# A recurrent attention feeding a two-layer MLP on one core: low input halves by a matmul with minus the identity, late checks in halves and spread out, a third output buffer

## The chip, the cores and the metric

The kernel runs on one core of a Trainium2 chip. The metric is the device time of one execution in microseconds (us). The engines are named as in the profile: PE (TensorE matmuls; PEld its weight loads), DVE (VectorE), ACT (ScalarE), POOL (GpSimd) and SP (the queue that issues all DMAs here).

## The reference

```python
def _attn_ref(r, k, v, w, u):                 # each of r, k, v, w: (4, 8, 768, 48); u: (8, 48)
    state = zeros((B, H, D, D))
    for t in range(S):
        cur = einsum('bhd,bhe->bhde', u[None] * kt, vt)
        y[:, :, t] = einsum('bhd,bhde->bhe', rt, state + cur)
        state = wt[:, :, :, None] * state + einsum('bhd,bhe->bhde', kt, vt)
    return y

def _moe_ref(x, w_in, w_out, alpha):          # x: (3072, 384), w_in: (384, 2048), w_out: (2048, 384)
    h = x @ w_in
    g = maximum(h, 0) + alpha * minimum(h, 0)
    return g @ w_out
```

The attention output, rows of 8 heads by 48, is the x of the MLP.

## The kernel before

The sequence is cut into 6 chunks of 128 steps for each of 4 batches, 24 chunks q in all. For a chunk, `prep` makes running products of the decays w on DVE (two scans, L359 and L365) and scales k and r with them (L368, L371); `scores` multiplies them on PE (L422), DVE lays the products below the diagonal into a tile `at` (L427, copy_predicated), whose diagonal ACT has written (L398); `outputs` adds the part of the carried state (L509) and `at` times v (L464), and updates the state (L471). The chunk's output, transposed, lies in a PSUM bank `yp`.

Three chunks make a group of 384 tokens, whose inputs x must be split in two 32-bit reduced-precision tiles, high and low, so that three products (high by high, low by high, high by low) give nearly full precision. `take` in `outputs` does this: ACT casts `yp` to the high tile (L484), DVE subtracts the high tile from `yp` to get the low one (L486). For groups after the first a part of 128 columns, `x3s`, is split in the same way and moved into place by six small DMAs (L538).

The MLP runs in steps. A step n takes one tile j of 128 hidden columns for one group: nine matmuls "up" (L588) into a bank; ACT scales (L592, "pos"), DVE combines (L594), ACT casts the high half (L596, "gh"), DVE the low half (L597, "gl"); two steps later (LAG = 2) nine matmuls "down" (L606), three each for the three chunks, add to PSUM tiles `op0` to `op2`. The weights are loaded as 16 tiles `raw`, and each is rebuilt and split into `wh` and `wl` by two ACT and four DVE instructions (L561, L563, L566, L569, L572, L574). There are 8 groups by 16 tiles, 128 steps. The first three groups run the tiles 0 to CUT - 1 first, and the rest later, so that work on PE begins before all weights are made; their partial sums go to DRAM (`part`) and are read back and added by L619.

The checks that the fast path may be used read all decays again (12 loads, L677; one ACT instruction each, L679) and all weights again (16 loads, L686; two ACT instructions each, L688 and L689). The sums of the last two come with a short extra instruction that reads the accumulator. They share the ring of two `raw` buffers. Their result is one number, read at the end.

What stands on each engine, and in which order, is decided when the kernel is built. `Plan.op` records each piece of work with an engine, an estimated duration, the tiles it reads and writes and, for some, a due time; `Plan.order` goes through time with these estimates and gives each free engine the ready piece with the earliest due time; buffers come from rings of fixed length. On the chip each engine then runs its list strictly in this order, waiting where data is late. `PLACE` says before which steps the chunks of the first three groups are due, `STEP` and `ATT` what a step and a chunk are taken to cost in the due times.

At the end, `moe_out` copies `op0` to `op2` of the last group to tiles `os` (a ring of two; ACT for s = 0 and 2, DVE for s = 1) and sends each to DRAM (L628):

```python
                os_ = Tensor(r_os)
                ...
                    op("ACT", 0.41, lambda s=s, os_=os_: nc.scalar.copy(out=os_.ap, in_=ops_[s]),
                       r=[("op", s)], w=[os_], due=due_step[n] + STEP)
```

## Time and profile before

| | us |
|---|---|
| median of 3 runs | 556.07 (553.01 to 557.01) |
| the profiled execution's own time | 559.03 |
| span of the profiled execution, first to last instruction | 557.3 |
| PE busy in the span | 527.0 (95%) |
| DVE busy | 356.4 (64%) |
| ACT busy | 311.7 (56%) |
| POOL busy | 60.0 (11%) |
| mean granted PE clock | 0.974 of full |

Busy time is a mean over a span whose stages differ, and PE's matmuls overlap each other, so a high share does not say that PE never waited. What a stage is bound by is read from that stage: which engine is without a gap there, and which wait of PE ends last.

### The profile page before, as it was taken

The numbers are of one execution on the slowest core, as the hardware profiler recorded it, in microseconds if no ns is written. First come the engines' busy times: TensorE is split into PE (matmuls) and PEld (weight loads), VectorE is DVE, ScalarE is ACT, GpSimd is POOL, SyncE is SP. The second block draws the span as 40 slices with busy tenths as digits, with TensorE's granted clock in tenths as the row PEclk, the third lists the DMA queues.
The fourth block names the chain that finished last, engine by engine and source line by source line (L and its number), as shares of the span: only waits on it lengthen the run. The fifth ranks groups of instructions, "written<-read, shape, count | busy, mean of one in ns | idle before, by whom it ended". The sixth has DMA issues, their size and how long they took to land.

```text
span 557.3 us, 9687 instructions
## 1 busy us (share of the span) xinstructions
PE 527.0 (95%) x3724; PEld 507.2 (91%) x3724; DVE 356.4 (64%) x604; ACT 311.7 (56%) x720; POOL 60.0 (11%) x74
## 2 busy tenths in 40 slices
PE   6977888999999999989999999999999999999993
PEld 6866777999999899979999999999999999999993
DVE  7999999999997464655646376466484434333331
ACT  3865665856667878687745545445454443333331
POOL 2002315410002010020100110110000000000000
PEclk9788998999999999989999999999999999999998
DMA  8666565655557878777604232223121100000001
GB/s 310 207 219 208 180 202 177 223 168 167 196 168 239 287 247 303 240 265 254 209 0 107 66 102 77 85 70 103 58 74 23 42 1 2 18 19 29 0 2 48
DMA packets 29655, 75.14 MB, mean 135 GB/s; under 512 B 4064, under 2 KB 10912, under 8 KB 29600
## 3 DMA queue, kind: packets, MB, share of 16 engines
q1 hardware_dynamic: 29600, 74.44, 41.2%
q8 instruction: 31, 0.51, 0.4%
q14 instruction: 24, 0.20, 0.1%
HBM read 65.87 MB, written 6.49 MB: 130 GB/s over the span
## 4 chain that ended last, share of the span: by engine, by line
PE 69%; DMA 11%; DVE 10%; ACT 5%; issue 2%; SPq 1%; DVEq 0%; ACTq 0%
PE bank L588 30%; PE op L606 29%; DMA raw<-in_wts_dram 7%; PE bank L422 3%; PE bank L464 2%; PE bank L509 2%; DMA out_dram<-os 2%; DVE wd L365 1%; ACT at L398 1%; DVE suf L359 1%; PE bank L471 1%; ACT raw L689 1%; DVE raw L569 1%; DMA u_dm<-in_u_dram 1%; DVE at L427 1%
## 5 line engine op out<-in xcount | busy, mean ns | idle before, releaser
L588 PE MATMUL bank<-x,wh 128*128 128x384 f32 x768 | 224.5, 347 | 1.7 <-ACT wh L572 0.9
L588 PEld LDWEIGHTS bank<-x,wh 128*128 128x128 f32 x768 | 143.7, 191 | 5.0 <-ACT wh L572 1.5
L592 ACT ACTIVATE pos<-bank,alpha_n 128x384 f32<-128x384 f32 x128 | 74.4, 581 | 120.1 <-PE bank L588 120.0
L606 PE MATMUL op<-wh,gh 128*128 128x384 f32 x384 | 132.4, 345 | 3.4 <-ACT gh L596 2.4
L588 PE MATMUL bank<-x,wl 128*128 128x384 f32 x384 | 132.1, 344 | 2.3 <-DVE wl L574 2.3
L606 PE MATMUL op<-wh,gl 128*128 128x384 f32 x384 | 131.7, 343 | 1.8 <-DVE gl L597 1.5
L606 PE MATMUL op<-wl,gh 128*128 128x384 f32 x384 | 130.8, 340 | 0.0
L594 DVE SCALAR_TENSOR_TENSOR pos<-bank,pos 128x384 f32<-128x384 f32 x128 | 70.8, 553 | 87.5 <-ACT pos L592 87.3
L597 DVE TENSOR_TENSOR gl<-pos,gh 128x384 fp32r<-128x384 f32 x128 | 75.6, 590 | 52.2 <-ACT gh L596 51.7
L596 ACT CAST gh<-pos 128x384 fp32r<-128x384 f32 x128 | 65.4, 511 | 51.9 <-DVE pos L594 51.7
L606 PEld LDWEIGHTS op<-wh,gh 128*128 128x128 f32 x384 | 73.0, 190 | 5.1 <-ACT gh L596 3.0
L606 PEld LDWEIGHTS op<-wh,gl 128*128 128x128 f32 x384 | 73.0, 190 | 4.1 <-DVE gl L597 3.8
L588 PEld LDWEIGHTS bank<-x,wl 128*128 128x128 f32 x384 | 73.3, 191 | 3.1 <-DVE wl L574 3.1
L606 PEld LDWEIGHTS op<-wl,gh 128*128 128x128 f32 x384 | 73.2, 191 | 0.0
L398 ACT ACTIVATE at<-ident,cd 128x128 f32<-128x128 f32 x192 | 60.9, 392 | 0.4
L427 DVE COPY_PREDICATED at<-mask,bank 128x512 f32<-128x512 int32 x48 | 32.9, 728 | 20.6 <-PE bank L422 20.3
L407 POOL TENSOR_TENSOR St<-St,pc_all 128x192 f32<-128x192 f32 x20 | 13.7, 686 | 287.7 <-ACT pc_all L374 287.7
L365 DVE TENSOR_TENSOR_SCAN wd<-wd,low 128x520 f32<-128x520 f32 x24 | 32.0, 1334 | 0.1
L359 DVE TENSOR_TENSOR_SCAN suf<-wd,low 128x520 f32<-128x520 f32 x24 | 29.6, 1232 | 3.9 <-POOL ones L306 3.7
L422 PE MATMUL bank<-kr 64*128 64x128 f32 x384 | 29.8, 292 | 0.4 <-ACT kn L443 0.2
L422 PEld LDWEIGHTS bank<-kr 64*128 64x128 f32 x384 | 24.8, 194 | 5.3 <-issue 3.1
L389 POOL TENSOR_TENSOR rk<-rk,u_bc 128x384 f32<-128x384 f32 x18 | 20.6, 1144 | 60.7 <-DMA rk<-in_nat_dram 41.5
(76 smaller groups left out, 475.7 us busy)
## 6 DMA issues: line engine op xcount, KB each, us to landing
raw<-in_wts_dram SPq DMA_DIRECT2D x32, 768.0 KB, 4.6
kr<-in_dmaj_dram SPq DMA_DIRECT2D x24, 512.0 KB, 4.0
rk<-in_nat_dram SPq DMA_DIRECT2D x18, 384.0 KB, 3.1
wd<-in_dmaj_dram SPq DMA_DIRECT2D x24, 260.0 KB, 2.8
raw<-in_dmaj_dram SPq DMA_DIRECT2D x12, 520.0 KB, 4.6
nv<-in_nat_dram SPq DMA_DIRECT2D x24, 256.0 KB, 4.1
out_dram<-os SPq DMA_DIRECT2D x24, 192.0 KB, 2.1
x<-x3s SPq DMA_DIRECT2D x42, 48.0 KB, 2.1
```

The lines of the kernel that those rows point to most:

```text
L359: op("DVE", 1.18, lambda: nc.vector.tensor_tensor_scan(out=suf.ap[:, ::-1], data0=w.ap[:, ::-1], data1=low[:, ::-1], initial=0.0, op0=ALU. ...
L365: op("DVE", 1.18, lambda: nc.vector.tensor_tensor_scan(out=w.ap, data0=w.ap, data1=low, initial=0.0, op0=ALU.mult, op1=ALU.max), r=["low"] ...
L389: op("POOL", 1.0, lambda i=i: nc.gpsimd.tensor_tensor(out=rk.ap[:, 0:HD], in0=rk.ap[:, 0:HD], in1=u_bc if i == 0 else rk.ap[:, HD:], op=AL ...
L398: nc.scalar.activation(out=at.ap[:, o, p, :], in_=ident, func=AF.Copy, scale=cd.ap[:, o * NP + p:o * NP + p + 1])
L422: nc.tensor.matmul(sps[o].ap[:, p * P:(p + 1) * P], lhsT=kr.ap[FULL[o], 0, p, :], rhs=kr.ap[FULL[o], 1, p, :], start=True, stop=True)
L427: op("DVE", 0.65, lambda o=o: nc.vector.copy_predicated(out=at.ap[:, o], mask=mask.unsqueeze(1).broadcast_to([P, NP, P]), data=pairs(sps[o ...
L588: nc.tensor.matmul(hp.ap[:, 0:GT], lhsT=a[:, j, 0, ks], rhs=x.ap[:, xi, k, :], start=(i == 0), stop=(i == 3 * KT - 1))
L592: op("ACT", 0.5, lambda: nc.scalar.activation(out=pos.ap, in_=hp.ap[:, 0:GT], func=AF.Relu, scale=alpha_n[:, j:j + 1]), r=[hp, "alpha"], w ...
L594: op("DVE", 0.55, lambda: nc.vector.scalar_tensor_tensor(out=pos.ap, in0=hp.ap[:, 0:GT], scalar=0.0, in1=pos.ap, op0=ALU.max, op1=ALU.subt ...
L596: op("ACT", 0.41, lambda: nc.scalar.copy(out=gh.ap, in_=pos.ap), r=[pos], w=[gh])
L597: op("DVE", 0.47, lambda: nc.vector.tensor_tensor(out=gl.ap, in0=pos.ap, in1=gh.ap.bitcast(F32), op=ALU.subtract), r=[pos, gh], w=[gl], lo ...
L606: nc.tensor.matmul(ops_[s], lhsT=a.ap[:, ts], rhs=w[:, j, 1, :], start=(j == j0 and i == 0), stop=(j == j1 - 1 and i == 2))
```

## The change

The change has these parts:

- For the first six chunks (LO_BY_PE = 6) the low tile is no longer made by DVE. A tile `minus` holds minus the identity; PE multiplies it with the high tile and adds the product to `yp`, which then holds the low part, and ACT casts it out. There are nine such matmuls, nine more ACT casts and nine fewer DVE subtractions.
- The diagonal pieces of a chunk on ACT (L398) are recorded as four pieces of two instructions instead of two of four.
- CUT is 6 instead of 7, and PLACE moves the chunks 4 and 5 one step later and the chunks 6 to 8 one earlier.
- Every late check's ACT instructions are cut in two halves, and its load may not be placed before a time of its own (`after`), from the due time of step 52 on in equal gaps.
- The planner takes PE to be 8% slower until 95 us of its time, adds 0.15 us to PE's and 0.03 us to the other engines' latency, and some estimates differ slightly.
- The third output of the last group is copied to a tile of the ring `r_pos` instead of waiting for one of the two of `r_os`.
- The up product of the third step from the end is due one step earlier.

```diff
-CUT = 7
+CUT = 6
-STEP = 3.13
+STEP = 3.15
-PLACE = {0: (-1, -1, -1), 1: (1, 2, 3), 2: (8, 9, 10)}
+PLACE = {0: (-1, -1, -1), 1: (1, 3, 4), 2: (7, 8, 9)}
...
+CHECK_FROM = 52
+LO_BY_PE = 6
+SLOW, SLOW_TO = 1.08, 95.0
...
-            o.left, o.ready = len(o.deps), 0.0
+            o.left, o.ready = len(o.deps), o.after
...
+                    dur *= SLOW if now < SLOW_TO else 1.0
...
-                    end += o.lat
+                    end += o.lat + (0.15 if e == "PE" else 0.03)
...
+        op("ACT", 0.2, lambda: nc.scalar.mul(out=minus, in_=ident, mul=-1.0), r=["ident"], w=["minus"])
...
                 for c0, dst, key, t in parts:
                     op("ACT", t, lambda c0=c0, dst=dst: nc.scalar.copy(out=dst(0), in_=src(c0)), r=[yp], w=[(key, (s, 0))])
+                if q < LO_BY_PE:
+                    def rests():
+                        for c0, dst, key, t in parts:
+                            nc.tensor.matmul(src(c0), lhsT=minus, rhs=dst(0), start=False, stop=True, skip_group_check=True)
+                    op("PE", 0.25 * len(parts), rests, r=["minus", *[(key, (s, 0)) for _, _, key, _ in parts]], w=[yp], kind="MM")
                 for c0, dst, key, t in parts:
+                    if q < LO_BY_PE:
+                        op("ACT", t, lambda c0=c0, dst=dst: nc.scalar.copy(out=dst(1), in_=src(c0)), r=[yp], w=[(key, (s, 1))])
+                        continue
                     op("DVE", t + 0.05, lambda c0=c0, dst=dst: nc.vector.tensor_tensor(
                         out=dst(1), in0=src(c0), in1=dst(0).bitcast(F32), op=ALU.subtract),
...
-                os_ = Tensor(r_os)
+                os_ = Tensor(r_os if q < NQ - 1 else r_pos)
...
+        begin = due_step[CHECK_FROM]
+        gap = (late - 20.0 - begin) / (NQ // 2 + NF)
+        def check_load(i, src, out):
+            op("SP", 0.4, lambda: nc.sync.dma_start(out=out(), in_=src), w=[(raw, 0), (raw, 1)], lat=2.0, due=late,
+               after=begin + i * gap)
...
-            op("ACT", 0.9, lambda w1=w1: nc.scalar.activation(out=w1(), in_=w1(), func=AF.Square), w=[raw])
-            op("ACT", 1.1, lambda j=j, w1=w1: nc.scalar.activation(out=w1(), in_=w1(), func=AF.Relu, scale=-1.0, bias=tiny[:, 0:1],
-                                                                   accum_out=wt_all[:, j:j + 1]), r=["tiny"], w=[raw, ("wt", j)])
+            for h in range(2):
+                w1 = lambda raw=raw, h=h: raw.ap[:, h * DM:(h + 1) * DM, 1].bitcast(F32)
+                op("ACT", 0.45, lambda w1=w1: nc.scalar.activation(out=w1(), in_=w1(), func=AF.Square), w=[(raw, h)])
+                op("ACT", 0.65, lambda j=j, h=h, w1=w1: nc.scalar.activation(
+                    out=w1(), in_=w1(), func=AF.Relu, scale=-1.0, bias=tiny[:, 0:1],
+                    accum_out=wt_all[:, 2 * j + h:2 * j + h + 1]), r=["tiny"], w=[(raw, h), ("wt", 2 * j + h)])
```

In the rows below a line number is that of the kernel it is taken from. Before and after the change, L588 and L605 are "up", L606 and L624 "down", L592 and L610 "pos" on ACT, L594 and L612 "pos" on DVE, L596 and L614 "gh", L597 and L615 "gl", L486 and L503 the subtraction for the low tile.

**DVE, up to the gl of step 14.** Before, the instructions that lead to the 14th gl stand like this:

```order
L566 SCALAR_TENSOR_TENSOR cx_100<-raw_98,cx_100 128x768
L594 SCALAR_TENSOR_TENSOR pos_120<-bank_76,pos_120 128x384
L569 ISA raw_98<-raw_98,cx_100 128x768x2
L597 TENSOR_TENSOR gl_125<-pos_120,gh_122 128x384
L368 TENSOR_TENSOR kr_103<-kr_103,suf_111 128x512
L574 TENSOR_TENSOR wl<-raw_98,wh 128x768
L594 SCALAR_TENSOR_TENSOR pos_121<-bank_79,pos_121 128x384
L563 TENSOR_SCALAR cx_100<-raw_99 128x768
L597 TENSOR_TENSOR gl_126<-pos_121,gh_123 128x384
```

After the change the same place reads:

```order
L580 TENSOR_SCALAR cx_101<-raw_99 128x768
L379 TENSOR_TENSOR kr_104<-kr_104,wd_103 128x512
L612 SCALAR_TENSOR_TENSOR pos_121<-bank_75,pos_121 128x384
L591 TENSOR_TENSOR wl<-raw_100,wh 128x768
L615 TENSOR_TENSOR gl_126<-pos_121,gh_123 128x384
L583 SCALAR_TENSOR_TENSOR cx_101<-raw_99,cx_101 128x768
L640 COPY os_129<-op_73 128x384
L612 SCALAR_TENSOR_TENSOR pos_122<-bank_79,pos_122 128x384
L586 ISA raw_99<-raw_99,cx_101 128x768x2
L615 TENSOR_TENSOR gl_127<-pos_122,gh_124 128x384
```

Counted over DVE's whole list, the 14th gl is instruction 172 before and 167 now: nine subtractions are gone, and four other instructions that came behind it (L379, L583, L586, L640 of the change: the scaling of r, two parts of a weight tile, an output copy) now stand ahead of it.

**ACT, around the pos of step 46.** Before, the weight checks (L688, L689) stand between the diagonal pieces (L398), the input casts (L484) and the step's own work:

```order
L596 CAST gh_124<-pos_120 128x384
L688 ACTIVATE raw_99<-raw_99 128x768
L689 ACTIVATE raw_99,wt_all<-raw_99,tiny 128x768
L411 COPY Sd<-St_93 64x4x48 x2
L398 ACTIVATE at_114<-ident,cd_112 128x128 x4
L484 CAST x_117<-bank_76 128x3x128
L592 ACTIVATE pos_121<-bank_75,alpha_n 128x384
L398 ACTIVATE at_114<-ident,cd_112 128x128 x4
L596 CAST gh_122<-pos_121 128x384
L484 CAST x3s_119<-bank_76 128x128
L688 ACTIVATE raw_98<-raw_98 128x768
L688 ACTIVATE raw_99<-raw_99 128x768
```

After, the same steps (45 to 48) have no check until the first half of a decay check (L703) in step 48:

```order
L610 ACTIVATE pos_121<-bank_76,alpha_n 128x384
L406 ACTIVATE at_115<-ident,cd_113 128x128 x4
L614 CAST gh_125<-pos_121 128x384
L492 CAST x3s_120<-bank_78 128x128
L610 ACTIVATE pos_122<-bank_79,alpha_n 128x384
L382 COPY pc_all<-suf_112 128x4
L614 CAST gh_123<-pos_122 128x384
L610 ACTIVATE pos_121<-bank_77,alpha_n 128x384
L451 COPY kn<-bank_75 128x4x112
L614 CAST gh_124<-pos_121 128x384
L610 ACTIVATE pos_122<-bank_76,alpha_n 128x384
L703 ACTIVATE raw_100,wv_all<-raw_100,m_one 128x520
```

Over the whole list the checks stood on ACT in the steps 27 to 54 and stand now in the steps 48 to 111, the weight checks (32 halves of each kind) in 76 to 111.

**PE, ahead of the first up product.** The added matmuls with `minus` of the chunks 1 and 2 stand like this, where nothing of the kind stood before:

```order
L430 MATMUL bank_79<-kr_104 128x128
L430 MATMUL bank_75<-kr_104 128x128
L497 MATMUL bank_76<-x_117,minus 128x384
L497 MATMUL bank_77<-x_117,minus 128x384
L479 MATMUL bank_78<-nv_111,kn 64x48 x8
L449 MATMUL bank_79<-ident,kr_104 128x112 x4
L605 MATMUL bank_76<-x_117,wh 128x384
```

The eight score matmuls of chunk 3 (L430, the last two of them shown) and one more matmul with `minus`, that of chunk 0, stand ahead of these. In the whole list the output of chunk 8 came ahead of the up product of step 11 and comes now ahead of that of step 10.

More of the change, by code (lines that the diff above doesn't have):

```diff
@@ L590, in products @@
                         i += 1
-            op("PE", STEP / 2, products, r=[("wh", j, 0), ("wl", j, 0), ("down", n - LAG - 1), *x_keys(g)], w=[hp, "up"], kind="MM", due=due_step[n] + STEP / 2)
+            op("PE", STEP / 2, products, r=[("wh", j, 0), ("wl", j, 0), ("down", n - LAG - 1), *x_keys(g)], w=[hp, "up"], kind="MM",
+               due=due_step[n] + STEP / 2 - (STEP if n == len(due_step) - LAG - 2 else 0))
             op("ACT", 0.5, lambda: nc.scalar.activation(out=pos.ap, in_=hp.ap[:, 0:GT], func=AF.Relu, scale=alpha_n[:, j:j + 1]),
@@ L671, in fast_path @@
         late = due_step[-1] - 20.0
+        begin = due_step[CHECK_FROM]
[3 more added lines that the diff above has]
+               after=begin + i * gap)
         for i in range(NQ // 2):
             raw = Tensor(r_raw)
-            v = lambda raw=raw: raw.ap.rearrange("p f t -> p (f t)")[:, 0:2 * SC].bitcast(F32)
-            op("SP", 0.4, lambda i=i, v=v: nc.sync.dma_start(
-                out=pairs(v(), SC), in_=dmaj[2 * i:2 * i + 2, :, 0:SC].rearrange("q p f -> p q f")), w=[raw], lat=1.5, due=late)
@@ L679, in fast_path @@
[L679 to L681 removed]
+            v = lambda raw=raw: pairs(raw.ap.rearrange("p f t -> p (f t)")[:, 0:2 * SC].bitcast(F32), SC)
+            check_load(i, dmaj[2 * i:2 * i + 2, :, 0:SC].rearrange("q p f -> p q f"), v)
+            for h in range(2):
+                op("ACT", 0.75, lambda i=i, v=v, h=h: nc.scalar.activation(
+                    out=v()[:, h], in_=v()[:, h], func=AF.Relu, bias=m_one[:, 0:1],
+                    accum_out=wv_all[:, 2 * i + h:2 * i + h + 1]), r=["m_one"], w=[(raw, h), ("wv", 2 * i + h)])
```

38 lines of the change are left out of this document (18 added, 20 removed).

## The prediction

> **What bounds the kernel now.** I read the page's slices first, then the busy time by stage.
>
> ```profile
> span 557.3 us, 9687 instructions
> DVE  7999999999997464655646376466484434333331
> ACT  3865665856667878687745545445454443333331
> ...
> 20.00:100.00 80.00, 67.31 (x593) 59.50 (x592) 77.43 (x120) 52.89 (x141) 19.85 (x17) 0.91 0.62 199
> 100.00:180.00 80.00, 80.00 (x527) 78.73 (x527) 75.24 (x121) 54.25 (x112) 13.32 (x12) 1.00 0.58 189
> 180.00:290.00 110.00, 105.67 (x729) 100.92 (x727) 61.66 (x112) 81.18 (x174) 11.94 (x14) 0.98 0.69 232
> 290.00:540.00 250.00, 250.00 (x1719) 245.54 (x1719) 123.26 (x225) 110.78 (x257) 11.96 (x14) 1.00 0.17 49
> ```
>
> The columns of a stretch are its length, then busy time of PE, PEld, DVE, ACT and POOL, the granted clock, and DMA. There are four stages. From 20 to 100 us DVE is the bound: 77.43 of 80 us, while PE has gaps. From 100 to 180 us PE has no gap, and DVE is nearly full too. From 180 to 290 us PE loses time again, DVE is half idle, and ACT is at its fullest, 81 of 110 us. From 290 us on PE is gapless, and nothing but fewer matmuls would help.
>
> How much PE loses from 180 to 290 us shows against a gapless stretch of the same length. The pairs of rows are the up matmuls (L588), the down matmuls (L606) and one matmul group of each chunk (L509, eight records a chunk):
>
> ```profile
> 180.00:290.00 110.00, 48.68 (x243) 0.98 0.69 232
> 300.00:410.00 110.00, 49.74 (x252) 1.00 0.27 79
> ...
> 180.00:290.00 110.00, 50.50 (x242) 0.98 0.69 232
> 300.00:410.00 110.00, 49.90 (x259) 1.00 0.27 79
> ...
> 180.00:290.00 110.00, 4.21 (x32) 0.98 0.69 232
> 300.00:410.00 110.00, 5.26 (x40) 1.00 0.27 79
> ```
>
> The gapless stretch did 9 + 17 = 26 more matmuls of the MLP and one more chunk. The chain that ended last gives their prices:
>
> ```profile
> 316.22 1.05 PE op L606 x6
> ...
> 320.75 1.76 PE bank L588 x9
> ```
>
> Six matmuls take 1.05 us, 0.175 each, and a chunk is put in between 317.27 and 320.75 us, 3.5 us. So **8.1 us** (26 x 0.175 + 3.5) are lost in the third stage. By the waits of PE from 165 to 300 us, the two largest are these:
>
> ```profile
> PE op L606 <- ACT gh L596: 2.4, 2, 2.0
> PE op L606 <- DVE os L619: 1.0, 2, 0.5
> ```
>
> And the worst place, ACT first, then PE:
>
> ```profile
> 238.30 0.90 ACT L688 ACTIVATE raw<-raw 128x768 f32<-128x768 f32 x1 [3.14 <-DMA raw<-in_wts_dram]
> ...
> 240.94 1.28 ACT L398 ACTIVATE at<-ident,cd 128x128 f32<-128x128 f32 x4
> ...
> 242.49 0.57 ACT L592 ACTIVATE pos<-bank,alpha_n 128x384 f32<-128x384 f32 x1
> ...
> 244.13 0.50 ACT L596 CAST gh<-pos 128x384 fp32r<-128x384 f32 x1
> ...
> 244.68 0.44 PE L606 MATMUL op<-wh,gh 128*128 128x384 f32 x1 [1.99 <-ACT gh L596]
> ...
> 246.21 0.52 PE L588 MATMUL bank<-x,wh 128*128 128x384 f32 x1
> ...
> 248.91 0.34 PE L606 MATMUL op<-wh,gh 128*128 128x384 f32 x1
> ```
>
> A weight check stands at the head of ACT's list and waits 3.14 us for its own load; a block of diagonals (240.94) and the step's pos (242.49) queue behind it, and PE stands 1.99 us for the gh. The clock then drops: the nine up matmuls from 246.21 to 248.91 us take 2.7 us instead of nine times 0.175, 1.1 us more.
>
> **The change, part by part.** The sum is made against the profiled execution, 559.03 us by its own time, 557.3 of span; the median is 556.07, so 3.0 us go off the result for the median.
>
> *Checks moved.* With none in the steps 27 to 47, the ACT waits of the third stage lose their cause. The waits for L619 (1.0 us: partial sums read back before a group's PSUM tile may be overwritten) stay. New is ACT work in a stage where ACT has 139 us free of 250. Halving adds fixed cost:
>
> ```profile
> L688 ACT ACTIVATE raw<-raw 128x768 f32<-128x768 f32 x16 | 14.4, 907 | 9.8 <-DMA raw<-in_wts_dram 9.8
> L484 ACT CAST x<-bank 128x384 fp32r<-128x384 f32 x24 | 11.4, 474 | 9.5 <-PE bank L464 9.4
> L484 ACT CAST x3s<-bank 128x128 fp32r<-128x128 f32 x21 | 5.6, 268 | 0.0
> ```
>
> Going by the 474 ns of a 384-wide cast, two halves cost 0.95 us for 0.907; with a second reading of the accumulator, 28 checks add a few us to ACT alone. From 290 us on ACT is busy 110.78 of 250 us, 1.4 us of each step of 3.15 (18 x 0.175), so a half of about 0.5 us (an estimate from the 474 ns) fits its gap. Bounds for new waits are 0 and the whole 8.1 us again. I take 0.8, nearest to the stage that is gapless now: the DMA share is 0.69 where the loads were and 0.17 where they go. On SP the 28 loads now stand among the moves of x3s and the outputs; a load whose buffer is not free holds those behind it, but with two buffers and 28 loads in 64 steps it should be free. Gain: 8.1 - 1.0 - 0.8 = **6.3 us**.
>
> The Trainium skill, page "TensorE: Matmul & The Clock Gate", Part 1, puts the fall to half clock after at least one idle window of about 3.4 us. Here a wait of 1.99 us is followed by slow matmuls, so the trace differs and decides. By the page that 1.1 us would not come from the wait and might stay; the gain would then be 5.2 us here and the total 1.1 us less.
>
> *Low parts by PE.* DVE loses nine subtractions, and by the order four other instructions came forward ahead of the 14th gl:
>
> ```profile
> L486 DVE TENSOR_TENSOR x<-bank,x 128x384 fp32r<-128x384 f32 x24 | 13.0, 542 | 6.6 <-ACT x L484 5.1 <-ACT x3s L484 1.5
> L486 DVE TENSOR_TENSOR x3s<-bank,x3s 128x128 fp32r<-128x128 f32 x21 | 5.7, 277 | 0.0
> L371 DVE TENSOR_TENSOR kr<-kr,wd 128x512 f32<-128x512 f32 x24 | 17.2, 718 | 0.0
> L566 DVE SCALAR_TENSOR_TENSOR cx<-raw,cx 128x768 int32<-128x768 int32 (+1 forms) x17 | 15.3, 903 | 0.0
> L569 DVE CUSTOM_DVE_ANT_0 raw<-raw,cx 128x1536 uint16<-128x1536 uint16 (+1 forms) x17 | 18.1, 1067 | 0.0
> L622 DVE COPY os<-op 128x384 f32<-128x384 f32 x8 | 4.4, 554 | 6.6 <-PE op L606 6.6
> ```
>
> Removed are 6 x 0.542 + 3 x 0.277 = 4.1 us, ahead of that gl come 0.718 + 0.903 + 1.067 + 0.554 = 3.2 us, so it stands only 0.8 us earlier in DVE's work. Why this gl decides: in the second stage it arrives as PE needs it.
>
> ```profile
> 120.45 0.56 DVE L597 TENSOR_TENSOR gl<-pos,gh 128x384 fp32r<-128x384 f32 x1
> ...
> 121.26 0.34 PE L606 MATMUL op<-wh,gl 128*128 128x384 f32 x1
> ```
>
> It ends at 121.01 us and is used at 121.26; PE cannot be further ahead there than 0.8 + 0.25 us, unless DVE also waits less. From 20 to 120 us its largest wait was this:
>
> ```profile
> DVE pos L594 <- ACT pos L592: 2.1, 3, 0.9
> ```
>
> From step 14 to the third stage PE is gapless, so what is won by then is kept and not more. I take **1.5 us**, between the bounds -3 (below) and 4.1 (all of the removed work). CUT and PLACE act through the same list: the scores of chunk 8 come earlier, but with one step fewer done, and the 14th gl counts both. The nine added matmuls cost 0.18 (spacing) to 0.35 us (one alone), 1.6 to 3.2 us of a PE that has 12.7 us free in the first stage; they would be paid only where PE is the bound. Nine casts, six of 0.474 and three of 0.268 us, add 3.6 us to ACT's 52.9 of 80. The risk is order: a matmul with `minus` waits at PE's head for ACT's high cast, with scores and up products queued behind it and DVE's masking behind the scores. Bound: three such waits of a block of diagonals each, with what follows about 1.5 us, take 4.5 from the 1.5 and make the -3.
>
> *The tail.*
>
> ```profile
> 548.56 0.33 PE L606 MATMUL op<-wl,gh 128*128 128x384 f32 x1
> 547.88 0.48 ACT L625 COPY os<-op 128x384 f32<-128x384 f32 x1 [1.40 <-PE op L606]
> 548.38 3.79 SPq L628 DMA_DIRECT2D out_dram<-os  x3
> 551.33 0.48 ACT L625 COPY os<-op 128x384 f32<-128x384 f32 x1 [2.98 <-DMA out_dram<-os]
> ```
>
> The third copy waits for the first output to land; with its own buffer it starts near 548.9 us, 2.4 us earlier. SP's three issues spread from 548.38 to 552.17, and if the second keeps SP until about 550.2 the third issue gains only 1.5 us. Bounds 0.6 and 2.4, taken **1.5**. The up product that is due earlier changes PE's order, not its work: nothing.
>
> The sum is 6.3 + 1.5 + 1.5 = 9.3 us: 549.7 for the profiled execution, and **546.8 us** as the median.
>
> **The rivals.** A measurement tells about 1% of this kernel, 5.6 us, from no change.
>
> *DVE's relief passes through.* If DVE's waits for pos vanish too, because scores and up products come earlier, the first stage gives the 4.1 us of the subtractions and up to 2.1 of waits, 4 to 6 us rather than 1.5: about 543. For it: the output of chunk 8 stands ahead of step 10 now. Against it: the 14th gl.
>
> *Checks take their waits along.* The halves are as many us of ACT as before, and one late load blocks everything behind it, as at 238.30 us. If 28 checks lose PE 0.29 us each as before (8.1 / 28), only early part and tail remain: 553. For it is the strict list; against it the low DMA share and wider spacing.
>
> *The matmuls with `minus` stall PE (slower).* If all six chunks make PE wait for two blocks of diagonals and the high cast, about 1.28 x 2 + 0.47 = 3 us each, the first stage loses 18 us against the 7.8 gained elsewhere: 566. It decides from about 13 us of loss on. Against it: ACT's high casts of the chunks 0 and 1 stand several instructions ahead of their use in the order.
>
> *The early reorder does nothing or harm.* Fewer weight tiles first, but the same DVE list: with the bound of -3, 551.
>
> **How the numbers follow.** Forecast (544.5 to 549.5) 0.52, relief passing through 0.15, checks taking their waits along 0.21, harmless early part 0.06, slower 0.06. Low end 541.5, the first rival's with 2.4 us in the tail; the high end 552.5 takes in half of the checks' rival; outside are about 2 in 10. Faster by over 1% (below 550.5) are the first two and a fifth of the third, 0.71; slower 0.06; the rest, 0.23, within.
>
> **What would show it.** PE busy by stage: the third should be gapless but for about 1.8 us, and 290 to 540 us too; waits of PE for gh there would confirm the second rival. No ACT wait for an output DMA at the end. In the second stage the gl should still arrive as PE needs it, with the first up product of step 14 about 1.5 us earlier. A wait of PE at the `minus` matmuls of over 1 us would make the early part wrong. If the clock drops where PE never waited, the 1.1 us was not the wait's.

## The result and the profile after

The changed kernel took **540.26 us** (median of 4, 538.70 to 541.68) against 556.07 us of the kernel before beside it: a ratio of 0.9727, 95% interval 0.9669 to 0.9786. A fourth execution of the kernel before took 2841.09 us and is left out of both numbers. Run again beside its variants the changed kernel gave 0.9689 (0.9654 to 0.9724). The profiled execution took 540.92 us by its own time, 539.1 of span, against 559.03 and 557.3 before. Forecast were 546.8 us, within 541.5 to 552.5, and a gain of 9.3; the measured time lies below the low end, and the two profiles are 18.1 us apart.

The page after, span and the slices of DVE and ACT:

```profile
span 539.1 us, 9763 instructions
...
DVE  5799999999995738665736566556474444333332
ACT  2677777765654346555646567668777675653332
```

ACT's full stretch in the middle has gone to the second half. The stages of the changed kernel, with the columns as in the prediction:

```profile
20.00:100.00 80.00, 72.39 (x687) 64.61 (x688) 76.16 (x122) 60.93 (x171) 20.13 (x19) 0.94 0.62 209
100.00:180.00 80.00, 78.98 (x497) 77.10 (x496) 71.69 (x114) 46.10 (x90) 8.66 (x9) 1.00 0.48 155
180.00:290.00 110.00, 110.00 (x819) 107.76 (x818) 66.97 (x119) 61.10 (x152) 13.81 (x15) 1.00 0.38 115
290.00:520.00 230.00, 229.70 (x1584) 225.36 (x1582) 115.36 (x212) 143.00 (x356) 11.35 (x14) 1.00 0.36 117
```

PE is without a gap from 180 to 290 us now (110.00, before 105.67), at a full clock (1.00, before 0.98).

Where the 18 us come from is read from four points that both programs pass: the first matmul of the 16th, 60th and 124th up product, and the last matmul of all. PE has done the same work by each of them in both kernels, but for the nine matmuls with `minus`. PE's instructions in time, first of before (its last matmul, at 548.56, stands in the prediction), then of after:

```profile
121.61 0.34 PE L588 MATMUL bank<-x,wh 128*128 128x384 f32 x1
...
291.40 0.34 PE L588 MATMUL bank<-x,wh 128*128 128x384 f32 x1
...
529.90 0.34 PE L588 MATMUL bank<-x,wh 128*128 128x384 f32 x1
```

```profile
118.48 0.33 PE L605 MATMUL bank<-x,wh 128*128 128x384 f32 x1
...
278.47 0.33 PE L605 MATMUL bank<-x,wh 128*128 128x384 f32 x1
...
514.62 0.33 PE L605 MATMUL bank<-x,wh 128*128 128x384 f32 x1
...
529.01 0.33 PE L624 MATMUL op<-wh,gh 128*128 128x384 f32 x1
...
532.99 0.34 PE L624 MATMUL op<-wl,gh 128*128 128x384 f32 x1
```

| stretch | before, us | after, us | won, us | forecast |
|---|---|---|---|---|
| to the 16th up product | 121.6 | 118.5 | 3.1 | 1.5 |
| 16th to 60th | 169.8 | 160.0 | 9.8 | 6.3 |
| 60th to 124th | 238.5 | 236.2 | 2.3 | 0 |
| 124th to the last matmul | 18.7 | 18.4 | 0.3 | 0 |
| last matmul to the end of the span | 8.7 | 6.1 | 2.6 | 1.5 |

The third line is the odd one. From the 60th up product on PE has next to no gap in either kernel (229.70 of 230 us after the change) and does the same matmuls, and still it is faster after the change. The tail of before shows it by itself: the 24th down matmul from the end starts here,

```profile
544.50 0.34 PE L606 MATMUL op<-wh,gh 128*128 128x384 f32 x1
```

and the last at 548.56, 23 distances in 4.06 us, 176.5 ns each. After the change it is 532.99 less 529.01 by 23, 173.0 ns. Over the neighbouring MLP matmuls from 300 to 525 us (1068 and 1084 pairs, chunks left out) the mean from start to start is 176.1 ns before and 173.4 after.

### The profile page after: what moved, and what is told of

The parts are those of the page before. It is cut to its first block, busy times and chain, and to the rows that moved or that the text cites. A ratio compares the mean times of both kernels' runs of the same rounds, so it can differ in the third digit from the quotient of the medians.

```text
span 539.1 us, 9763 instructions
## 1 busy us (share of the span) xinstructions
PE 518.3 (96%) x3733; PEld 501.0 (93%) x3733; DVE 348.4 (65%) x595; ACT 324.2 (60%) x802; POOL 56.9 (11%) x74
## 4 chain that ended last, share of the span: by engine, by line
PE 74%; DVE 14%; DMA 5%; issue 3%; ACT 2%; SPq 1%; DVEq 0%; ACTq 0%
PE bank L605 30%; PE op L624 30%; PE bank L430 4%; DMA raw<-in_wts_dram 4%; PE bank L472 3%; PE bank L526 3%; DVE gl L615 2%; DVE raw L586 2%; DVE wd L373 2%; DVE wl L591 1%; PE bank L479 1%; DMA u_dm<-in_u_dram 1%; DVE cx L583 1%; DVE at L435 1%; PE bank L390 1%
## 5 line engine op out<-in xcount | busy, mean ns | idle before, releaser
L605 PE MATMUL bank<-x,wh 128*128 128x384 f32 x768 | 218.9, 339 | 3.2 <-ACT kn L451 1.8
L605 PEld LDWEIGHTS bank<-x,wh 128*128 128x128 f32 x768 | 140.5, 188 | 6.2 <-ACT kn L451 2.1
L610 ACT ACTIVATE pos<-bank,alpha_n 128x384 f32<-128x384 f32 x128 | 74.1, 579 | 98.6 <-PE bank L605 97.5
L624 PE MATMUL op<-wh,gl 128*128 128x384 f32 x384 | 129.5, 337 | 3.3 <-DVE gl L615 3.3
L624 PE MATMUL op<-wh,gh 128*128 128x384 f32 x384 | 129.8, 338 | 0.0
L624 PE MATMUL op<-wl,gh 128*128 128x384 f32 x384 | 129.0, 336 | 0.0
L605 PE MATMUL bank<-x,wl 128*128 128x384 f32 x384 | 128.5, 335 | 0.2 <-DVE wl L591 0.2
L612 DVE SCALAR_TENSOR_TENSOR pos<-bank,pos 128x384 f32<-128x384 f32 x128 | 70.5, 551 | 80.5 <-ACT pos L610 80.1
L615 DVE TENSOR_TENSOR gl<-pos,gh 128x384 fp32r<-128x384 f32 x128 | 74.9, 585 | 52.1 <-ACT gh L614 51.9
L614 ACT CAST gh<-pos 128x384 fp32r<-128x384 f32 x128 | 65.4, 511 | 54.2 <-DVE pos L612 54.0
L624 PEld LDWEIGHTS op<-wh,gl 128*128 128x128 f32 x384 | 72.5, 189 | 4.9 <-DVE gl L615 4.8
L624 PEld LDWEIGHTS op<-wh,gh 128*128 128x128 f32 x384 | 72.4, 189 | 0.6
L605 PEld LDWEIGHTS bank<-x,wl 128*128 128x128 f32 x384 | 72.1, 188 | 0.5 <-DVE wl L591 0.5
L624 PEld LDWEIGHTS op<-wl,gh 128*128 128x128 f32 x384 | 72.5, 189 | 0.0
L406 ACT ACTIVATE at<-ident,cd 128x128 f32<-128x128 f32 x192 | 62.8, 392 | 0.9 <-PE bank L472 0.4
L415 POOL TENSOR_TENSOR St<-St,pc_all 128x192 f32<-128x192 f32 x20 | 11.5, 577 | 260.1 <-ACT pc_all L382 253.0
L373 DVE TENSOR_TENSOR_SCAN wd<-wd,low 128x520 f32<-128x520 f32 x24 | 30.8, 1282 | 0.0
L430 PE MATMUL bank<-kr 64*128 64x128 f32 x384 | 29.7, 297 | 0.8 <-DVE kr L379 0.8
L430 PEld LDWEIGHTS bank<-kr 64*128 64x128 f32 x384 | 24.9, 199 | 4.9 <-issue 3.6
```

What stands on the lines that cost most here:

```text
L373: op("DVE", 1.15, lambda: nc.vector.tensor_tensor_scan(out=w.ap, data0=w.ap, data1=low, initial=0.0, op0=ALU.mult, op1=ALU.max), r=["low"] ...
L406: nc.scalar.activation(out=at.ap[:, o, p, :], in_=ident, func=AF.Copy, scale=cd.ap[:, o * NP + p:o * NP + p + 1])
L430: nc.tensor.matmul(sps[o].ap[:, p * P:(p + 1) * P], lhsT=kr.ap[FULL[o], 0, p, :], rhs=kr.ap[FULL[o], 1, p, :], start=True, stop=True)
L605: nc.tensor.matmul(hp.ap[:, 0:GT], lhsT=a[:, j, 0, ks], rhs=x.ap[:, xi, k, :], start=(i == 0), stop=(i == 3 * KT - 1))
L610: op("ACT", 0.5, lambda: nc.scalar.activation(out=pos.ap, in_=hp.ap[:, 0:GT], func=AF.Relu, scale=alpha_n[:, j:j + 1]), r=[hp, "alpha"], w ...
L612: op("DVE", 0.55, lambda: nc.vector.scalar_tensor_tensor(out=pos.ap, in0=hp.ap[:, 0:GT], scalar=0.0, in1=pos.ap, op0=ALU.max, op1=ALU.subt ...
```

## The experiments

Eighteen runs were made, of which ctrl and after_again repeat the two kernels unchanged. Two small parts of the change have no run of their own: the diagonal pieces recorded in four, and the up product due one step earlier. "Last" is the start of the last matmul in the profile, "spacing" the mean start to start of MLP matmuls from 300 to 525 us.

| kernel | median, us | ratio to before, 95% interval | last, us | spacing, ns |
|---|---|---|---|---|
| ctrl | 558.64 | (one run) | 548.0 | 176.1 |
| tail | 556.22 | 0.9979 (0.9949 to 1.0008) | 549.7 | 176.1 |
| chk_new | 546.67 | 0.9805 (0.9762 to 0.9848) | 535.9 | 173.4 |
| chk_old | 550.72 | 0.9879 (0.9827 to 0.9931) | 542.2 | 176.1 |
| gap_x | 554.46 | 0.9946 (0.9920 to 0.9971) | 547.1 | 174.4 |
| gap_all | 557.26 | 0.9999 (0.9974 to 1.0023) | 547.6 | 176.1 |
| gap96 | 555.48 | 0.9941 (0.9908 to 0.9974) | 546.6 | 173.5 |
| after_gap | 542.61 | 0.9746 (0.9703 to 0.9789) | 534.2 | 174.3 |
| after128 | 543.81 | 0.9740 (0.9706 to 0.9773) | 536.2 | 175.8 |
| early_only | 545.90 | 0.9773 (0.9738 to 0.9808) | 537.1 | 173.5 |
| lo0 | 546.75 | 0.9848 (0.9794 to 0.9902) | 537.2 | 173.4 |
| place | 547.18 | 0.9795 (0.9769 to 0.9821) | 538.3 | 173.4 |
| after_again | 541.35 | 0.9689 (0.9654 to 0.9724) | 533.1 | 173.4 |
| est_old | 541.47 | 0.9701 (0.9655 to 0.9747) | 534.0 | 173.4 |
| whole2 | 541.02 | 0.9694 (0.9650 to 0.9737) | 533.1 | 173.4 |
| pool_half | 551.37 | 0.9878 (0.9835 to 0.9920) | 540.3 | 176.1 |
| u9 | 543.24 | 0.9745 (0.9700 to 0.9789) | 535.3 | 173.4 |
| u12 | 548.58 | 0.9866 (0.9809 to 0.9923) | 539.6 | 173.4 |

### Each part of the change by itself

**ctrl**, the kernel before, unchanged.

> The kernel before, unchanged, profiled once more. The open point is the stage from 300 us on, where PE is gapless in both kernels, yet a matmul of the MLP follows the one ahead of it after 176.0 ns on the mean in the profile before and after 173.4 ns in that after the change, which is worth some 2.4 us over the last 64 steps. If that is a property of one execution or of the chip it ran on, this run can show 173 to 174 ns and a time near 553 to 554 us. If it belongs to the kernel before, it shows 175.8 to 176.3 ns again and 556 us.

It showed 176.1 ns again: the spacing belongs to the kernel.

**tail**, the kernel before with

```diff
-                os_ = Tensor(r_os)
+                os_ = Tensor(r_os if q < NQ - 1 else r_pos)
```

> The kernel before with the third output's own buffer alone; the lists of PE and DVE are the same word for word. By the prediction's term 1.5 us less, with the bounds 0.6 and 2.4. By the comparison of the two profiles 2.6 us less: from the start of the last matmul to the end of the span it is 8.74 us before and 6.11 after, and the third copy would start about 0.4 us behind the last matmul instead of 2.8. The spacing of the matmuls from 300 us on should stay what the control shows.

The end of this kernel in time, and then that of the changed kernel:

```profile
549.50 2.02 SPq L628 DMA_DIRECT2D out_dram<-os  x2
...
549.68 0.33 PE L606 MATMUL op<-wl,gh 128*128 128x384 f32 x1
550.11 0.48 ACT L625 COPY pos<-op 128x384 f32<-128x384 f32 x1 [0.63 <-PE op L606]
551.61 0.45 SPq L628 DMA_DIRECT2D out_dram<-pos  x1
```

```profile
532.83 1.03 SPq L646 DMA_DIRECT2D out_dram<-os  x2
...
533.42 0.48 ACT L643 COPY pos<-op 128x384 f32<-128x384 f32 x1 [0.62 <-PE op L624]
533.96 0.41 SPq L646 DMA_DIRECT2D out_dram<-pos  x1
```

In both the third copy no longer waits for an output. In tail alone the two issues ahead keep SP until 551.5, and the third starts 1.9 us after the last matmul started; in the changed kernel they end at 533.9 and it starts after 1.0. From the last matmul to the end of the span (556.7 in tail) it is 7.0 us in tail and 6.1 in the changed kernel, against 8.7. The changed kernel's first profile is the best of its kind: in the 13 profiles with the third buffer this stretch takes 6.1 to 7.3 us, mean 6.8, in the seven without it 8.4 to 8.9, mean 8.7. So the part is worth some 1.9 us, 1.7 in tail and up to 2.6; the times say 1.2 (less than 0 to 2.8).

**chk_new** is the kernel before with the new checks and their `after` times; **chk_old** is the changed kernel with the block of checks of before.

> The kernel before with the late checks in halves and spread out, and nothing else of the change; the orders are the same as before up to about step 30. The prediction's term is 6.3 us less (8.1 lost in the third stage, 1.0 of waits for L619 kept, 0.8 of new waits). By the comparison of the two profiles it is 8 to 9 us less, with no wait of PE for gh from 180 to 290 us. The rival that the checks take their waits along gives under 2 us. If the checks also set the spacing of the matmuls from 300 us on (by what stands on ACT or by the DMA there), it goes from 176 to 173.4 ns and a further 2.4 us come off: 10 to 11 us in all.

> The changed kernel with the late checks as before, whole and early; the orders are those of the changed kernel up to about step 30. If the early part is worth what the comparison of the profiles says, the first up product of step 16 stands at 118.5 us as in the changed kernel (121.6 before), and the time is 540.3 plus the 8 to 9 us of the checks: 548 to 550. By the prediction's terms it would be 540.3 plus 6.3: 546.6. The spacing from 300 us on stays at 173.4 ns if the checks do not set it, and is 176 if they do.

chk_new gained 10.9 us, as much as checks and spacing together were to give, and its spacing was 173.5 ns on the mean already from 100 to 180 us (176.1 in the kernel before), where its orders are still those of before and no late check has run. chk_old had 176.1 ns with all of the early edits. So the spacing came with the check edit, but not by what ACT or the loads do. What else the edit alters is size: wt_all grows from 64 to 128 bytes per partition, wv_all from 48 to 96, and all tiles allocated behind them move, x, gh and gl among them, while wh and wl stay. These lines of the change, which the extract under "The change" does not show, set the two sizes and add `minus`:

```diff
+        minus = const.tile([P, P], F32R, name="minus")
...
-        wt_all = const.tile([P, NF], F32, name="wt_all")
+        wt_all = const.tile([P, 2 * NF], F32, name="wt_all")
...
-        wv_all = const.tile([P, NQ // 2], F32, name="wv_all")
+        wv_all = const.tile([P, NQ], F32, name="wv_all")
```

### The distance in SBUF

**gap_x** is the kernel before with one unused tile ahead of x,

```diff
+        gap32 = const.tile([P, 8], F32, name="gap32")
         r_x = ring("x", [P, 2, KT, GT], 3, F32R)
```

**gap_all** has it ahead of wh instead, so that all of them move together, and **after_gap** is the changed kernel with it ahead of x.

> The kernel before with an unused tile of 32 bytes per partition allocated ahead of x, and no other edit: every engine's list is that of before, and x, pos, gh, gl and os lie 32 bytes further on. The two control profiles and the two partial changes say that the spacing of the MLP's matmuls is 173.4 ns where the check tiles wt_all and wv_all have the new sizes, and 176.0 where they have the old ones, from 100 us on, long before the first late check runs. The new sizes move x, gh and gl from a multiple of 64 bytes to 32 bytes behind one, where wh and wl also stand. Theory of the address: 173.4 ns here, and 117 gapless steps of 18 matmuls by 2.6 ns, 5.5 us less. Theory of the checks (what ACT or the loads do): 176.0 ns and no change.

> The kernel before with the same unused 32 bytes ahead of wh, so that all tiles move: wh and wl then lie on a multiple of 64 bytes, x, gh and gl 32 bytes behind one. If the address of x, gh and gl by itself decides, the spacing is 173.4 ns and the time 5.5 us less. If it is the place of the one operand against the other (both at 32 behind a multiple of 64 is good, one at 0 and one at 32 is bad), the spacing stays 176.0 ns and the time that of before.

> The changed kernel with the unused 32 bytes ahead of x, so that x, gh and gl are back on a multiple of 64 bytes while wh and wl are not. Theory of the address: the spacing goes from 173.4 to 176.0 ns, and the time from 540.3 to 545 to 546 us. Theory of the checks: nothing changes, 540.3 us. If the former holds, this is what the change would have measured without its accident, and the prediction's sum (546.8) is to be held against it.

gap_all settles that one operand's place against the other's counts: x, gh and gl moved as in gap_x, but wh moved too, and nothing changed (0.9999, 176.1 ns). gap_x and after_gap hit neither of the forecast spacings, 174.4 and 174.3 ns, so the theory of 64 bytes was wrong. By the distance from wh to x modulo 256, the remainder of its division by 256, all of them fall in line, and two kernels were made to test that: **gap96** (`[P, 24]` instead of `[P, 8]` in gap_x) and **after128** (`[P, 32]` in the changed kernel). By the tile sizes, each taken up to a multiple of 32, x lies 165280 bytes behind wh in a partition before the change and 165888 after it.

> The kernel before with an unused tile of 96 bytes per partition ahead of x, so that x, gh and gl stand exactly where they stand in the kernel with the new checks alone, and no other edit. So far a matmul of the MLP takes 173.4 ns where the distance from wh to x is a multiple of 256 bytes (the changed kernel, the new checks alone), 174.3 at 32 and at 192 over one, 176.0 at 160 over one (before, and again when wh and x are moved together). Theory of the distance: 173.4 ns here, and 2.6 ns by 18 by 114 steps from the step 14 on, 5.3 us less than before. Theory that the checks have a part in it as well: 174 ns or more, under 4 us.

> The changed kernel with 128 unused bytes ahead of x: the distance from wh to x is 128 over a multiple of 256. If the distance matters modulo 256, this is as far off as can be, the spacing is 176 ns or more and the time 545 to 547 us. If it matters modulo 128, this is the same place as that of the changed kernel: 173.4 ns and 540.3.

The first and last of the same 24 down matmuls at the end, of gap96 and of after128:

```profile
542.64 0.33 PE L607 MATMUL op<-wh,gh 128*128 128x384 f32 x1
...
546.63 0.34 PE L607 MATMUL op<-wl,gh 128*128 128x384 f32 x1
```

```profile
532.16 0.34 PE L625 MATMUL op<-wh,gh 128*128 128x384 f32 x1
...
536.21 0.34 PE L625 MATMUL op<-wl,gh 128*128 128x384 f32 x1
```

That is 3.99 by 23, 173.5 ns, without any edit but 96 unused bytes, and 4.05 by 23, 176.1 ns, in the changed kernel pushed off. The spacing of after128 came out as expected; its time, 543.81 us, lies below the 545 to 547 expected.

| distance from wh to x, modulo 256 bytes | kernels | spacing, ns |
|---|---|---|
| 0 | after, chk_new, gap96, early_only | 173.4 to 173.5 |
| 32 | after_gap | 174.3 |
| 192 | gap_x | 174.4 |
| 128 | after128 | 175.8 |
| 160 | before, ctrl, gap_all, chk_old | 176.1 |

The table names the kernels that test it; all others stand in it by their own distance, 0 or 160. Each distance at 0, 32, 128, 160 and 192 modulo 256 was also at 0, 32, 128, 416 and 448 modulo 512, so the runs do not tell 256 from 512, and other remainders were not tried. Why PE is slower at some of them no run shows. It is PE that is slower: DVE's pos takes 556 ns and ACT's gh 511 or 512 from 300 to 500 us in before and in gap96.

gh and gl lie at the same remainder as x, and wl as wh, so up and down matmuls were moved together. The traces tell them apart all the same. In an up matmul wh or wl is the weight and x moves; in a down matmul gh or gl is the weight and wh or wl moves. The up product and the nine down matmuls that follow it, of gap_x:

```profile
535.27 0.33 PE L589 MATMUL bank<-x,wh 128*128 128x384 f32 x1
...
536.68 0.33 PE L589 MATMUL bank<-x,wh 128*128 128x384 f32 x1
536.86 0.33 PE L607 MATMUL op<-wh,gh 128*128 128x384 f32 x1
...
538.24 0.34 PE L607 MATMUL op<-wl,gh 128*128 128x384 f32 x1
```

Eight distances take 1.41 us up and 1.38 down, 176 and 172.5 ns. From 300 to 525 us an up matmul follows another after 175.6 ns on the mean in gap_x, a down matmul another after 172.9; in after_gap it is 173.8 and 174.5, and at 0, 128 and 160 the two differ by less than 0.5. So 174.4 at 192 and 174.3 at 32 are means of unlike matmuls, and gap_x has the slow spacing up and the fast one down. The Trainium skill, page "SBUF — State Buffer", section "Who interferes with whom", gives PE one read port for the moving operand and an independent one for the weight load, and says that PE never waits on anyone; these spacings, which hang on the two places together, differ from it, and decide.

In time gap96 won 3.3 us (1.4 to 5.1), not 5.3: in the third stage PE waits for ACT and DVE in that order of work, and a faster matmul only waits longer. From the 60th to the 124th up product it took 235.7 us, 2.8 less than before. Between after128 and the changed kernel the last matmul differs by 3.2 us.

### The checks and the early part

**early_only** is chk_old with 96 unused bytes ahead of x; **whole2** is the changed kernel with

```diff
-            for h in range(2):
-                op("ACT", 0.75, lambda i=i, v=v, h=h: nc.scalar.activation(
-                    out=v()[:, h], in_=v()[:, h], func=AF.Relu, bias=m_one[:, 0:1],
...
+            for h in range(1):
+                op("ACT", 1.35, lambda i=i, v=v, h=h: nc.scalar.activation(
+                    out=v(), in_=v(), func=AF.Relu, bias=m_one[:, 0:1],
...
```

and likewise for the weight checks.

> The changed kernel with the late checks as they were, whole and early, and 96 unused bytes ahead of x that keep the distance from wh to x a multiple of 256. It holds the early part, the tail and the address, not the checks. If the terms add up, it is before less 5.3 (address), 3.5 to 4 (early) and 1.8 to 2.6 (tail): 10.6 to 11.9 us less, a ratio of 0.979 to 0.981. If what the early part wins is lost again in the third stage, since the checks still block ACT there, under 9 us less.

> The changed kernel with the late checks spread out but whole, one ACT instruction instead of two halves; the result tiles keep their sizes, and x its distance from wh. If spreading carries the third stage, within 1 us of the changed kernel. If the halves are needed, since a whole weight check of 0.9 us does not fit the gaps of ACT from 290 us on, PE waits for gh there and 2 to 5 us are lost.

whole2 equals the changed kernel: spreading carries the third stage, halving adds nothing. early_only gained 12.7 us. With gap96 (no part but the distance), early_only and chk_new (early part or checks added) there are three corners of the third stage at one spacing; its row in each, in this order:

```profile
180.00:290.00 110.00, 104.73 (x729) 100.16 (x729) 63.17 (x116) 82.36 (x175) 14.12 (x15) 0.98 0.70 235
```

```profile
180.00:290.00 110.00, 106.84 (x782) 101.26 (x781) 71.56 (x127) 82.28 (x183) 19.67 (x18) 1.00 0.68 227
```

```profile
180.00:290.00 110.00, 110.00 (x818) 107.76 (x817) 67.49 (x120) 58.85 (x149) 14.29 (x15) 1.00 0.42 131
```

PE does 729, 782 and 818 matmuls in these 110 us, small ones of the chunks among them. Moving the checks fills the stage (110.00); the early part fills some of it with the old checks still there (106.84). The waits of PE in it, of gap96 and of early_only, say how:

```profile
PE op L607 <- ACT gh L597: 2.1, 2, 1.9
PE op L607 <- DVE gl L598: 2.1, 5, 1.2
PE op L607 <- DVE os L620: 1.1, 2, 0.6
```

```profile
PE op L625 <- DVE gl L616: 1.3, 3, 0.7
PE op L625 <- DVE os L638: 1.2, 1, 1.2
```

With the other early order no gh came late any more. So the two parts win some of the same time. By the last matmul, one profile each, the checks are worth 10.7 us on the old early part (546.6 to 535.9) and 4.0 on the new one (537.1 to 533.1); the early part 9.5 with the old checks and 2.8 with the new. By the ratios, over more executions, the checks are worth 7.6 us (0.9941 less 0.9805) and 4.7 (0.9773 less 0.9689): the same direction, but with an interval of about 2 us on each ratio these times alone would not show it. The rows of the stage do.

**lo0** is the changed kernel with `LO_BY_PE = 0`, **place** with `CUT = 7` and the PLACE of before, **est_old** with the planner's estimates of before (`SLOW` 1.0, no added latency, `STEP` 3.13, the old durations).

> The changed kernel with LO_BY_PE at 0, so that DVE makes the low parts of the first six chunks again; CUT, PLACE, the checks and the tail stay changed, and so do the addresses. The prediction gave the whole early part 1.5 us, by 4.1 us of subtractions less 3.2 us of other work moved ahead. The profiles say 3.1 to 4.0 us at step 16. If the subtractions carry it, this kernel loses 3 to 4 us against the changed one: 543.5 to 544.5. If the new places and the planner's constants carry it, it stays within 1 us of 540.3.

> The changed kernel with CUT 7 and PLACE as before, all else changed, the addresses too. If the early gain is that of the subtractions taken from DVE, within 1 us of the changed kernel's ratio of 0.9727. If it comes from fewer weight tiles ahead of the first groups, 2 to 4 us slower, a ratio of 0.976 to 0.980. In either case the excess of DVE's instructions up to the 14th gl over their undisturbed durations (11 to 12 us in the profiles with the order of before, 6 to 7.5 with that of the changed kernel) tells whether the order decides what POOL disturbs.

> The changed kernel with the planner's estimates of before: no slower PE until 95 us, no added latencies, STEP 3.13, the old durations of the scans and of the masking copies. Theory that the estimates keep DVE and POOL apart on the chip, since the planner never lets two of their locked pieces run at once by its own clock: the excess up to the 14th gl goes back to 9 us or more, and the time up by 2 to 5 us, a ratio of 0.977 to 0.983. Rival, that the removed subtractions and the new places do it: the excess stays at 6 to 8 us and the ratio at that of the changed kernel.

est_old keeps the ratio, 0.9701, so the theory that the estimates keep DVE and POOL apart fell. Each of the other two was 5 to 7 us slower than the changed kernel by its median, lo0 by more than its expectation had, and by the last matmul (537.2 and 538.3) both were even later than chk_new (535.9), which has neither: fewer subtractions on DVE and the new places pay only together. They lose in different places. lo0 starts its 16th up product at 118.7 us, as early as the changed kernel (118.5), and PE waits later, 1.6 us for gl and 1.5 for a copy of an output tile from 118 to 520 us; place starts it at 124.2, as late as the kernel before. By one profile each, the new places bring the gain up to there, and with the subtractions left on DVE it is lost again behind.

**pool_half** asks what slows DVE early. It is the kernel before without the second of POOL's two products for each chunk from chunk 6 on:

```diff
-                    op("POOL", 1.0, lambda i=i: nc.gpsimd.tensor_tensor(
-                        out=rk.ap[:, 0:HD], in0=rk.ap[:, 0:HD], in1=u_bc if i == 0 else rk.ap[:, HD:], op=ALU.mult),
+                    op("POOL", 1.0, lambda i=i: i == 0 and nc.gpsimd.tensor_tensor(
+                        out=rk.ap[:, 0:HD], in0=rk.ap[:, 0:HD], in1=u_bc, op=ALU.mult),
```

> The kernel before, with the second of the two products that POOL makes for each chunk from the sixth on left out (the output is then not the reference's); the planner still reckons with it, so the lists of all other engines are the same word for word. Theory of the contention: DVE's excess up to the 14th gl falls from 11 to 12.5 us to 6 to 8, and the first up product of step 16 comes 3 to 5 us earlier than in the profiles with the order of before (121.6 to 125.5 us), at 118 to 120. Rival, that DVE's excess comes from elsewhere, from loads that land in SBUF or from ACT: it stays at 11 to 12 us and step 16 within 1.5 us.

The 16th up product came at 116.8 us:

```profile
116.82 0.34 PE L588 MATMUL bank<-x,wh 128*128 128x384 f32 x1
```

DVE's groups from 0 to 120 us, by shape, of before, of the changed kernel and of pool_half:

```profile
L569 DVE CUSTOM_DVE_ANT_0 raw<-raw,cx 128x1536 uint16<-128x1536 uint16 x8 | 10.4, 1298 | 0.0
L597 DVE TENSOR_TENSOR gl<-pos,gh 128x384 fp32r<-128x384 f32 x13 | 9.9, 763 | 0.1
L368 DVE TENSOR_TENSOR kr<-kr,suf 128x512 f32<-128x512 f32 x10 | 7.5, 751 | 0.0
L371 DVE TENSOR_TENSOR kr<-kr,wd 128x512 f32<-128x512 f32 x9 | 7.0, 775 | 0.0
```

```profile
L615 DVE TENSOR_TENSOR gl<-pos,gh 128x384 fp32r<-128x384 f32 x14 | 9.4, 674 | 0.0
L586 DVE CUSTOM_DVE_ANT_0 raw<-raw,cx 128x1536 uint16<-128x1536 uint16 x9 | 8.8, 981 | 0.0
...
L379 DVE TENSOR_TENSOR kr<-kr,wd 128x512 f32<-128x512 f32 x10 | 6.8, 682 | 0.0
L376 DVE TENSOR_TENSOR kr<-kr,suf 128x512 f32<-128x512 f32 x10 | 6.8, 675 | 0.0
```

```profile
L597 DVE TENSOR_TENSOR gl<-pos,gh 128x384 fp32r<-128x384 f32 x15 | 11.1, 740 | 0.2
L569 DVE CUSTOM_DVE_ANT_0 raw<-raw,cx 128x1536 uint16<-128x1536 uint16 x9 | 9.2, 1026 | 0.0
...
L371 DVE TENSOR_TENSOR kr<-kr,wd 128x512 f32<-128x512 f32 x10 | 6.8, 683 | 0.0
L368 DVE TENSOR_TENSOR kr<-kr,suf 128x512 f32<-128x512 f32 x10 | 6.7, 675 | 0.0
```

Half of POOL's products gone, with every other engine's list unchanged, makes three of these four about as much shorter as the change makes them (1298 to 1026 and 981 ns, 751 to 675 both, 775 to 683 and 682); gl gains less (763 to 740 and 674). Taking each instruction up to the 14th gl against the shortest tenth of its kind, the excess is 10.9 to 12.5 us in the profiles with the order of before, 6.2 in pool_half, 5.8 to 7.6 with the changed order, 8.4 in place and 2.9 in lo0 (within 0.3 us, by how the shortest tenth is taken). The Trainium skill has, in the same section of "SBUF — State Buffer", a DVE instruction with two SBUF inputs contend with a GpSimd instruction that reads SBUF; this run agrees. Why the changed order collides less is not settled: POOL's products take nearly as long as before (27 us by then against 28 to 29), and no estimate explains it.

**u9** and **u12** ask whether more can be had: the changed kernel with `U_BY_PE` at 9 and at 12.

> The changed kernel with U_BY_PE at 9: the sums over r, u and k of the chunks 6 to 8 are made on PE (eight small matmuls, 1.05 us a chunk) from one DVE product, instead of two POOL products and a DVE reduction. If DVE's contention with POOL still bounds the early part, the excess up to the 14th gl falls from 6.5 us to 4 or less and the kernel gains 1 to 3 us, a ratio of 0.964 to 0.967. If PE bounds it by now, the three chunks add 3 us of PE work and the kernel loses 0 to 3 us, a ratio of 0.969 to 0.974.

> The same with U_BY_PE at 12: six chunks more on PE, those of the chunks 9 to 11 after step 14, where PE had no gap in the changed kernel. By that these three cost 1.05 us each whatever the chunks 6 to 8 bring: 3 us slower than u9. If DVE or POOL still bounds anything there, less than that.

Neither gained. u9's ratio is 0.9745, and its excess stayed at 6.4 us although POOL was busy for 15.5 us instead of 27: other instructions met what was left. In its first stage,

```profile
20.00:100.00 80.00, 73.84 (x705) 65.45 (x706) 77.17 (x121) 59.03 (x162) 9.20 (x10) 0.97 0.58 192
```

DVE is as full as ever with POOL down from 20.13 to 9.20 us. u12 lost 6.7 us more than u9 (0.9866 less 0.9745), twice what its PE work explains; the rest is open. Its excess was 1.6 us, with 5 us of POOL's products by then, so collisions are not what slows it. No variant is faster than the changed kernel, run again as **after_again**; est_old and whole2 equal it.

> The changed kernel once more, beside its variants on the same chip: 0.970 to 0.976 of before, the spacing 173.4 ns again, and the first up product of step 16 between 117 and 120 us. If its first profile was a lucky one, the ratio is nearer to 0.98.

## Why the prediction was wrong, step by step

**"From 290 us on PE is gapless, and nothing but fewer matmuls would help."** This is the largest of the steps that failed. The spacing of 0.175 us was taken as PE's own price and was a price of where tiles lie: before stood at a distance of 160 modulo 256 bytes, and `minus` (512 bytes) with the two larger check tiles moved x by 608 bytes, to 0. From the 60th up product on that is 2.6 of the 18.1 us (2.3 and 0.3). Between the 16th and the 60th after128 took 161.4 us against the 160.0 of the changed kernel (160.3 in after_again), 1.4 more: about 4.0 in all, where gap96 won 3.3 in time (1.4 to 5.1). That is enough to take the result out of the range: after128, the same change without the good distance, has 0.9740 of before, 541.6 us on 556.07, inside the range, though by less than its interval leaves open. The prediction put this term at nothing, with no reason but that PE is gapless, and no view of one profile could show it; the sizes of the tiles in the diff could have raised the question. That the new sizes met a good distance was luck, not design.

**Low parts by PE, 1.5 us.** The mechanism was half right. The list was 0.8 us shorter by the forecast, and is 1.0 shorter by undisturbed durations. The failed part is the pricing of DVE's instructions by fixed means: up to the 14th gl they lost 5 us less to what POOL's work costs them, and DVE waited some 2 us more elsewhere. In the seven profiles with the order of before the 16th up product starts at 121.6 to 125.5 us, mean 122.9; in the seven with the changed order at 117.3 to 119.2, mean 118.3. That is 4.6 us, above the bound of 4.1 (the two profiles of the sum have 3.1). Nor did the removed subtractions set the gain up to there: lo0 keeps them on DVE, with some 4 us more undisturbed work up to the 14th gl, and is as early, while place has them removed and is late. The rival of a relief that passes through had the size, not the cause: it saw waits for pos vanish. The matmuls with `minus` were as forecast: one wait of 0.8 us, among PE's waits from 60 to 100 us,

```profile
PE op L624 <- DVE gl L615: 1.4, 1, 1.4
PE bank L605 <- DVE at L435: 1.2, 1, 1.2
PE bank L497 <- ACT x3s L492: 0.8, 1, 0.8
```

and the rival that they stall PE is out.

**Checks, 6.3 us.** The loss of 8.1 was read right and went entirely: PE's 110.00 of 110 leave no room for the 1.0 us of L619, which was to stay, nor for the 0.8 of new waits. From the 16th to the 60th up product 9.8 us were won, 8.4 without the spacing, and part of it the early part would have won alone. The rival that the checks take their waits along is out; so is a need for halves. The fixed cost of the halves did go to ACT alone: from 290 to 520 us it is 143.00 us busy, 136.27 in whole2, and whole2 is no faster.

**The clock.** The prediction put 1.1 us of half clock down to a wait of 1.99 us, against the Trainium skill, page "TensorE: Matmul & The Clock Gate", Part 1, whose window of about 3.4 us would let the slow matmuls stay. The wait is gone and the granted clock of that stage is 1.00: by that the trace agrees with the wait as the cause. chk_new shows the same at 1.00 and gap96, with its gh wait of 1.9, 0.98. The trace of before also has the stretches in which half the clock was granted; the one here is 3.41 us long, and the 3.41 us ahead of it and the stretch itself read:

```profile
241.86:245.27 3.41, 1.28 (x6) 0.71 (x4) 1.97 (x5) 3.41 (x11) 0.00 (x0) 1.00 0.94 376
245.27:248.68 3.41, 3.27 (x10) 3.28 (x11) 3.05 (x6) 3.41 (x7) 0.12 (x1) 0.50 0.71 192
```

Ahead of the half clock PE was busy for 1.28 of 3.41 us, not idle throughout as that rule has it. Four more such stretches of before, from 33 to 92 us, followed 3.41 us in which PE was busy for 33 to 54% and had no gap longer than 2.3 us.

**The tail, 1.5 us.** Measured 1.7 alone, 1.9 on the mean of all profiles with and without it, and 2.6 between the two profiles of the sum, which is above the bound of 2.4 by luck of that one profile; the doubt about SP's second issue was the right one, and it varies.

**The sum.** For the two profiled executions: spacing 4.0, early 3.1, checks 8.4, tail 2.6, 18.1 us, where 0, 1.5, 6.3 and 1.5 stood. Nearly half of the 8.8 us that were missing is the spacing; the rest is early part, checks and tail, all three sized too small.

## What to carry to other kernels

A gapless PE can still be slow: compare the spacing of its matmuls between two profiles before taking it as fixed, and when an edit changes the size of any tile, ask what moved behind it; an unused tile of a few bytes is the cheapest control. On DVE beside a busy POOL, count the instructions by their undisturbed durations and the collisions apart, since a new order changes the second without a sign in the list. And parts of a change that relieve the same stage don't add: run each with and without the other.

## What the hardware showed that was not expected

- A matmul of 128x384 in the MLP follows the one ahead after 173.4 ns where the distance from wh to x leaves 0 modulo 256 bytes, 175.8 at 128 and 176.1 at 160: 3 to 4 us of this kernel. At 192 up matmuls take 175.6 and down matmuls, whose operands change parts, 172.9; at 32 it is 173.8 and 174.5.
- DVE's instructions met by POOL's products: 1298 ns on the mean for the 128x1536 16-bit one in the kernel before, 1026 with half of the products left out.
- Half the clock was granted for 3.41 us after 3.41 us in which PE was busy for 33 to 54% (five times in the kernel before between 33 and 249 us), with no gap longer than 2.3 us.
- With the same lists of work the 16th up product varies by 4 us between profiles (121.6 to 125.5), and the last matmul by 2.1 in those that also have the spacing of before (547.6 to 549.7): the third stage takes up part of what the first one lost.
